# Reading x^T turned straight from HBM, with the first weights on a second DMA queue, at the start of a fused attention and MLP kernel

## The chip, the cores and the metric

The kernel runs on one core of a Trainium2 chip. The metric is device time in microseconds (us) of one execution; the median of several executions is quoted. A profile adds records of one execution, and its own span is shorter than the device time of the same execution (260.0 against 261.42 us for the kernel before).

## The reference, cut to what matters

A linear-attention block and an MLP block read the same x (2048 tokens by 640), and a sigmoid gate mixes them. Only the first products matter here:

```python
x = A_x                                            # 1 x 2048 x 640, bf16
g = sigmoid((x * gate_w).sum(-1, keepdims=True))
qkv = x @ wqkv                                     # q, k, v of 640 columns each
pq, pk = phi(q), phi(k)                            # phi(t) = where(t > 0, t + 1, exp(t)) + 1e-6
...
return g * a + (1 - g) * b
```

The kernel computes q = x @ wq with x^T (features on partitions) as the stationary operand: in the trace of the kernel before, the q and k steps load 128x128 blocks of xT (LDWEIGHTS, 98 ns in the median) and multiply them with 512 and 128 to 131 columns of wq or wkg. In all, 16 tiles of 128 tokens must be turned.

## The kernel before

The program puts the loads of the start on SyncE's one queue, in about the order of need (a tiny "touch" of the weights on ScalarE's queue apart). Tiles 0 to 3 of x come plain and are turned by TensorE (five 128x128 transposes a tile, then a VectorE copy out of PSUM). Tiles 4 to 15 are turned by DMA transposes that read x_tok in SBUF.

```python
dma_in(x_tok[:, 0, :], x2[0:128, :], "x0")         # dma_in: SyncE's queue
dma_in(x_tok[:, 1, :], x2[128:256, :], "x1")
load_wq(0)
dma_in(x_tok[:, 2:4, :], x2[256:512, :].rearrange("(n p) d -> p n d", p=128), "x23")
for k in range(1, KD):                             # KD = 5 slices of 128 rows
    load_wq(k)
for k in range(KD):
    dma_in(wkg[:, k, 0:D], A_wqkv[128 * k:128 * (k + 1), D:2 * D], "wk%d" % k)
dma_in(wkg[:, :, D + 2:D + 3], gate_w..., "gw", noncontig=True)
for c in range(1, NCH):
    dma_in(x_tok[:, 4 * c:4 * c + 4, :], ..., "xc%d" % c)
    for t in range(4 * c, 4 * c + 4):
        sch.dma("sp", xT[:, :, 128 * t:128 * (t + 1)], x_tok[:, t, :], "trx%d" % (t % 4), transpose=True)
```

TensorE fills the wait for the first data with a warm-up of dummy matmuls, then interleaves transposes and the steps (tile, k) of q, so that no step needs a slice of wq long before it lands:

```python
WARM = 3200                                        # columns of dummy matmuls
addA(("warm",), 0.0, lambda: warmup(WARM, 0.834))
... transposes of tiles 0 and 1, two more dummies ...
order = [(0, 0), (None, None), (1, 0), (2, None), (3, None), (0, 1), (1, 1), (2, 0), (0, 2), (1, 2), (3, 0),
         (0, 3), (1, 3), (0, 4), (2, 1), (1, 4), (2, 2), (2, 3), (2, 4), (3, 1), (3, 2), (3, 3), (3, 4)]
```

Here (t, None) is the turning of tile t and (None, None) a dummy. After q of tiles 0 to 3 comes k of tile 0 in five steps, and then k of tile 1, which is the first tile of the ordinary kind; its start serves below as the end of the lead-in.

## Time and profile before

| | before |
|---|---|
| median time | 262.2 us (261.58 to 262.69, 4 runs) |
| TensorE busy | 254.7 of 260.0 us |
| first ordinary k tile starts | 12.6 us |
| from there to the end of the span | 247.4 us |

The page's span, its line of TensorE (PE; busy us, share of the span, instructions), and the first line of the chain that ended last:

```profile
span 260.0 us, 4263 instructions
PE 254.7 (98%) x1671; PEld 135.9 (52%) x1703; DVE 148.9 (57%) x266; ACT 106.9 (41%) x215; POOL 96.8 (37%) x151
...
PE 97%; issue 1%; DVE 1%; POOL 0%; POOLq 0%
```

The view of waits for TensorE (who waited for whom: us in total, times, longest):

```profile
PE ps L830 <- POOL xn L659: 1.1, 1, 1.1
PE ps L1106 <- issue: 0.5, 3, 0.2
```

TensorE is the limit, and beyond 0.5 us of issue it waits for nothing but the memset that feeds its warm-up. So there is little to win but the lead-in. The timeline shows that lead-in (start us, us, engine, line, operation, out<-in, shape, count, idle time before):

```profile
1.05 2.85 PE L830 MATMUL ps<-xn 128*128 128x512 bf16 x7 [1.05 <-POOL xn L659]
3.69 1.21 PE L611 MATMUL ps<-ident,x_tok 128*128 128x128 bf16 x10
...
5.11 0.38 PE L857 MATMUL ps<-wq,xT 128*128 128x512 bf16 x1
...
7.14 0.38 PE L857 MATMUL ps<-wq,xT 128*128 128x512 bf16 x1
7.41 0.38 PE L857 MATMUL ps<-wq,xT 128*128 128x512 bf16 x1
...
12.63 4.26 PE L600 MATMUL ps<-wkg,xT 128*128 128x512 bf16 x29
```

L830 is the warm-up, L611 the transposes, L857 the 512-column part of a q or k step (the other 128 columns follow). A duration of 0.38 us and a spacing of 0.27 us between steps are full speed here: the clock records of this trace put the rise to a granted clock of 1.00 at 4.7 us. The 25 steps before the ordinary k tile make 25 x 0.27 = 6.8 us, so 5.8 us of the 12.6 are lead-in.

The table of stretches (us; busy us and instructions of TensorE, its weight load, VectorE, ScalarE and GpSimd; last three columns: granted TensorE clock, DMA share, GB/s) shows the DMA engines full with plain loads from 4 us on:

```profile
4.00:6.00 2.00, 1.90 (x23) 1.49 (x21) 0.96 (x2) 0.00 (x0) 0.26 (x3) 1.00 1.03 350
6.00:8.00 2.00, 2.00 (x22) 1.29 (x20) 0.89 (x2) 0.00 (x0) 0.00 (x0) 1.00 1.04 340
```

The DMA transposes of this kernel, all from SBUF (durations of issue in ns, then us from issue to landing):

```profile
L281 SPq DMA_TRANSPOSE xT<-x_tok x12: 1200/1276/1595, 13.2 to 39.2; - x12
...
DMA to landing us min/median/max: 2.6/3.7/6.6
```

### The profile page before, as it was taken

What the parts mean: (1) busy time and instruction counts of PE and PEld (TensorE: products, weight loads), DVE (VectorE), ACT (ScalarE), POOL (GpSimd) and SP (SyncE); (2) the same over time, 40 slices, a digit from 0 to 9 for tenths busy, and PEclk for the clock granted to TensorE, in tenths of its full rate; (3) what the DMA queues carried; (4) which work ended last, traced back from release to release, by engine and by line L of the source; (5) the groups of instructions that cost most, each with busy time, mean ns of one, the idle gap of its engine ahead of it and who ended that gap; (6) DMA issues with size and microseconds to landing.
All of it is one profiled execution on the core that took longest, in us unless ns stands there. A gap on an engine that the chain in (4) does not pass through costs nothing.

```text
span 260.0 us, 4263 instructions
## 1 busy us (share of the span) xinstructions
PE 254.7 (98%) x1671; PEld 135.9 (52%) x1703; DVE 148.9 (57%) x266; ACT 106.9 (41%) x215; POOL 96.8 (37%) x151
## 2 busy tenths in 40 slices
PE   8999999999999999999999999999999999999996
PEld 4555555555555454555444545554455544455553
DVE  1597877899903799979994407992033410143333
ACT  1496777741355757674874240005500045100000
POOL 5013995859874017865854202230011100021001
PEclk9999999999999999999999999999999999999999
DMA  6855989642566894355565700232000020000311
GB/s 199 255 103 143 211 149 158 194 87 23 105 126 103 275 377 94 76 101 58 107 124 109 125 0 0 45 85 74 3 0 0 3 101 0 3 0 0 103 50 50
DMA packets 50691, 24.82 MB, mean 95 GB/s; under 512 B 42052, under 2 KB 49261, under 8 KB 50672
## 3 DMA queue, kind: packets, MB, share of 16 engines
q1 hardware_dynamic: 49280, 21.15, 35.8%
q0 software_dynamic: 1152, 3.28, 5.2%
q8 instruction: 13, 0.21, 0.3%
q10 hardware_dynamic: 240, 0.13, 0.2%
q14 instruction: 6, 0.05, 0.1%
HBM read 12.05 MB, written 2.62 MB: 56 GB/s over the span
## 4 chain that ended last, share of the span: by engine, by line
PE 97%; issue 1%; DVE 1%; POOL 0%; POOLq 0%
PE ps L600 61%; PE ps L1106 21%; PE ps L781 8%; PE ps L857 2%; PE ps L830 1%; PE ps L1020 1%; PE ps L1088 1%; DVE x_tok L639 1%; PE ps L858 1%; PE ps L611 1%; PE ps L934 1%; PE ps L1085 0%; POOL xn L659 0%; POOLq L1249 0%
## 5 line engine op out<-in xcount | busy, mean ns | idle before, releaser
L600 PE MATMUL ps<-xnT,w 128*128 128x512 bf16 x349 | 80.7, 379 | 0.5
L1106 PE MATMUL ps<-w,h2T 128*128 128x128 bf16 (+1 forms) x409 | 57.9, 298 | 0.7 <-issue 0.5
L656 ACT ACTIVATE h2T<-ps 128x512 bf16<-128x512 f32 x52 | 30.5, 600 | 65.6 <-PE ps L600 65.5
L600 PEld LDWEIGHTS ps<-xnT,w 128*128 128x128 bf16 x360 | 33.9, 98 | 36.9 <-issue 0.4
L639 DVE SCALAR_TENSOR_TENSOR x_tok<-ps,stg,abx 128x512 bf16<-128x512 f32 (+1 forms) x32 | 17.2, 551 | 61.6 <-PE ps L1106 61.6
L622 POOL TENSOR_SCALAR abx<-x_tok,stg 128x640 f32<-128x640 bf16 x16 | 14.8, 923 | 100.6 <-DVE x_tok L639 95.1
L1106 PEld LDWEIGHTS ps<-w,h2T 128*128 128x128 bf16 x416 | 32.4, 98 | 25.6 <-issue 1.1
L622 POOL TENSOR_SCALAR xn<-x_tok,st 128x640 bf16<-128x640 bf16 x32 | 36.8, 1155 | 15.4 <-DMA xnT<-xn 14.9
L656 ACT ACTIVATE Er<-ps 128x640 bf16<-128x640 f32 x32 | 22.4, 704 | 17.4 <-PE ps L600 8.5
L655 ACT ACTIVATE junk<-x_tok 128x640 bf16<-128x640 bf16 x32 | 23.6, 737 | 4.9 <-DVE x_tok L637 4.4
L656 ACT ACTIVATE hsT<-ps 128x512 bf16<-128x512 f32 (+1 forms) x32 | 18.9, 593 | 15.1 <-PE ps L600 12.7
L600 PE MATMUL ps<-w,hsT 128*128 128x512 bf16 (+1 forms) x159 | 23.8, 298 | 0.1
L600 PE MATMUL ps<-M_sb,pqnT 128*128 128x128 bf16 (+1 forms) x156 | 23.5, 297 | 0.3
L781 PE MATMUL ps<-pk_tok,x_tok 128*128 128x128 bf16 (+1 forms) x156 | 23.3, 297 | 0.2
L639 DVE SCALAR_TENSOR_TENSOR abx<-ps,stg,abx 128x640 f32<-128x640 f32 x16 | 14.1, 884 | 15.3 <-PE ps L600 15.3
L600 PE MATMUL ps<-wkg,xT 128*128 128x512 bf16 (+1 forms) x147 | 22.3, 298 | 0.2
L600 PEld LDWEIGHTS ps<-w,hsT 128*128 128x128 bf16 x160 | 13.3, 98 | 12.3
L600 PEld LDWEIGHTS ps<-M_sb,pqnT 128*128 128x128 bf16 x160 | 13.1, 98 | 10.4
L600 PE MATMUL ps<-wq,xT 128*128 128x512 bf16 (+1 forms) x119 | 18.2, 298 | 0.1
L622 DVE TENSOR_SCALAR Er<-Er 128x640 bf16<-128x640 bf16 x32 | 12.0, 376 | 9.1 <-ACT Er L656 8.8
L637 DVE SCALAR_TENSOR_TENSOR x_tok<-ps,x_tok 128x640 bf16<-128x640 f32 x16 | 13.1, 821 | 6.9 <-PE ps L600 6.0
L600 PEld LDWEIGHTS ps<-wkg,xT 128*128 128x128 bf16 x150 | 12.2, 97 | 9.0
(71 smaller groups left out, 230.0 us busy)
## 6 DMA issues: line engine op xcount, KB each, us to landing
w<-in_B_w_dram SPq DMA_DIRECT2D x1, 2160.0 KB, 8.2
w<-in_B_w_dram SPq DMA_DIRECT2D x1, 2080.0 KB, 13.7
x_tok<-in_A_x_dram SPq DMA_DIRECT2D x3, 640.0 KB, 5.7
out_dram<-x_tok SPq DMA_DIRECT2D x3, 640.0 KB, 3.5
w<-in_B_w_dram POOLq DMA_DIRECT2D x8, 160.0 KB, 4.8
wq<-in_A_wqkv_dram SPq DMA_DIRECT2D x5, 160.0 KB, 3.8
wkg<-in_A_wqkv_dram SPq DMA_DIRECT2D x5, 160.0 KB, 3.9
wv<-in_A_wqkv_dram POOLq DMA_DIRECT2D x1, 800.0 KB, 6.2
```

The costliest lines, as they stand in the source:

```text
L600: ins = e.matmul(out_ap, l, r, start=(i == 0), stop=(i == n - 1))
L611: ins = e.transpose(o, s_, ident[:])
L622: return engf(lambda e: e.tensor_scalar(out_ap, in_ap, s1, s2, op0, op1), rd, [out_ap], cost=cost)
L637: return dve(lambda e: e.scalar_tensor_tensor(out_ap, in0, scalar, in1, op0, op1, accum_out=accum), rd, [out_ap, accum], cost=cost + 70.0)
L639: return dve(lambda e: e.scalar_tensor_tensor(out_ap, in0, scalar, in1, op0, op1), rd, [out_ap], cost=cost)
L655: return act(lambda e: e.activation(out_ap, in_ap, func, bias=bias, scale=scale, accum_out=accum), rd, wr, cost=cost)
L656: return act(lambda e: e.activation(out_ap, in_ap, func, bias=bias, scale=scale), rd, wr, cost=cost)
L781: ins = e.matmul(o, l, r, start=(t0 + q_ == 0), stop=(t0 + q_ == NT - 1))
L830: ins = e.matmul(ps[:, b, 0:n], xn[:, 0, 0:128], xn[:, 0, 0:128].unsqueeze(1).to_broadcast([128, n // 128, 128]), start=True, stop=True)
L857: e.matmul(ps[:, b, 0:512], l, w[:, k, 0:512], start=(k == 0), stop=(k == KD - 1))
L858: return e.matmul(ps[:, b + 1, 0:n2], l, w[:, k, 512:512 + n2], start=(k == 0), stop=(k == KD - 1))
L1106: ins = e.matmul(o, l, r, start=False, stop=(i == KFF - 1), skip_group_check=(n0 > 0))
```

## The change

The intent is to take x's turning off TensorE altogether: all 16 tiles are read turned from HBM on SyncE's queue, wq and wk go out beside them on ScalarE's queue, and x itself follows behind, since only later work needs it. The warm-up reads a constant set before the start barrier; the gate's column is turned by a tiny matmul. Cut to its core:

```diff
-    dma_in(x_tok[:, 0, :], ...) ... load_wq ... wk ... xc ... trx from x_tok
+    def load_w(dst, name, k, c0):
+        sch.dma("act", dst[:, k, 0:D], A_wqkv[128 * k:128 * (k + 1), c0:c0 + D], "%s%d" % (name, k))
+    def x_turned(t):
+        sch.dma("sp", xT[:, :, 128 * t:128 * (t + 1)], x2[128 * t:128 * (t + 1), :], "trx%d" % (t % 4), transpose=True)
+    sch.dma("pool", gwr[0:KD, :], gate_w.rearrange("(k p) -> k p", p=128), "gw")
+    for t in range(4):
+        x_turned(t)
     for k in range(KD):
-        dma_in(wkg[:, k, 0:D], ...)
+        load_w(wq, "wq", k, 0)
+    for k in range(KD):
+        load_w(wkg, "wk", k, D)
+    for c in range(NCH):
+        x_chunk(c)
+        for t in range(4 + 3 * c, 7 + 3 * c):
+            x_turned(t)
...
-    WARM = 3200
-    WARM2 = 256
+    WARM = 3712
...
-        order = [(0, 0), (None, None), (1, 0), (2, None), (3, None), (0, 1), ... ]
+        order = [(t, k) for t in range(4) for k in range(KD)]
+        order.insert(KD, (None, None))             # here: the gate's matmul
```

More of the change, by code (lines that the diff above doesn't have):

```diff
@@ L464, in psb @@
         return ps[:, b, :].bitcast(BF16)[:, n0:n1]
-    ones_c = pa.alloc("ones_c", [128, 768], BF16)
+    ones_c = pa.alloc("ones_c", [128, 128], BF16)
     ident = pa.alloc("ident", [128, 128], BF16)
@@ L470, in _build @@
     negh = pa.alloc("negh", [128, 4], F32)
+    gwr = pa.alloc("gwr", [8, 128], BF16)
     st1 = pa.alloc("st1", [128, 8, NT], F32)
@@ L674, in dma_in, with x_chunk @@
         return sch.dma("sp", out_ap, in_ap, key, **kw)
-    sch.dma("act", junk[0:16, 0, 0:80].rearrange("p (k f) -> p k f", k=KD),
-            A_wqkv[:, 0:16].rearrange("(k e r) f -> e r k f", k=KD, r=8)[:, 0, :, :], "touch")
-    dma_in(x_tok[:, 0, :], x2[0:128, :], "x0")
-    dma_in(x_tok[:, 1, :], x2[128:256, :], "x1")
-    def load_wq(k):
-        dma_in(wq[:, k, :], A_wqkv[128 * k:128 * (k + 1), 0:D], "wq%d" % k)
-    load_wq(0)
-    dma_in(x_tok[:, 2:4, :], x2[256:512, :].rearrange("(n p) d -> p n d", p=128), "x23")
-    for k in range(1, KD):
-        load_wq(k)
-    for k in range(KD):
-        dma_in(wkg[:, k, 0:D], A_wqkv[128 * k:128 * (k + 1), D:2 * D], "wk%d" % k)
-    dma_in(wkg[:, :, D + 2:D + 3], gate_w.rearrange("(k p o) -> p k o", p=128, o=1), "gw", noncontig=True)
-    for c in range(1, NCH):
-        dma_in(x_tok[:, 4 * c:4 * c + 4, :], x2[512 * c:512 * (c + 1), :].rearrange("(n p) d -> p n d", p=128), "xc%d" % c)
-        for t in range(4 * c, 4 * c + 4):
-            sch.dma("sp", xT[:, :, 128 * t:128 * (t + 1)], x_tok[:, t, :], "trx%d" % (t % 4), transpose=True)
+    def load_w(dst, name, k, c0):
+        sch.dma("act", dst[:, k, 0:D], A_wqkv[128 * k:128 * (k + 1), c0:c0 + D], "%s%d" % (name, k))
+    def x_turned(t):
+        sch.dma("sp", xT[:, :, 128 * t:128 * (t + 1)], x2[128 * t:128 * (t + 1), :], "trx%d" % (t % 4), transpose=True)
+    def x_chunk(c):
+        dma_in(x_tok[:, 4 * c:4 * c + 4, :], x2[512 * c:512 * (c + 1), :].rearrange("(n p) d -> p n d", p=128), "xc%d" % c)
+    sch.dma("pool", gwr[0:KD, :], gate_w.rearrange("(k p) -> k p", p=128), "gw")
+    for t in range(4):
+        x_turned(t)
+    for k in range(KD):
+        load_w(wq, "wq", k, 0)
[5 more added lines that the diff above has]
+            x_turned(t)
     k_done = {}
@@ L716, in load_wvo @@
             sch.dma("pool", wo_aug[0:n, r, :], A_wo[R6 * r:R6 * r + n, :], "wo", group_total=6, deps=dp)
-    memset(pool, xn[:, 0, 0:128], 1.0)
     memset(pool, ones_c[:], 1.0)
@@ L740, in _build, with gate_turn @@
     IT = _Items()
-    WARM = 3200
-    WARM2 = 256
-    def t_x(t):
+    WARM = 3712
+    def gate_turn():
         b = bank()
-        tr_group(b, [x_tok[:, t, 128 * k:128 * (k + 1)] for k in range(KD)])
-        src = psb(b, 0, D).rearrange("p (k c) -> p k c", k=KD)
-        dst = xT[:, :, 128 * t:128 * (t + 1)]
-        copy(dve, dst, src)
+        pe(lambda e: e.matmul(ps[:, b, 0:KD], gwr[0:KD, :], ident[0:KD, 0:KD], start=True, stop=True),
+           [gwr[0:KD, :], ident[:]], [ps[:, b, 0:KD]], cost=60.0)
+        copy(dve, wkg[:, :, D + 2:D + 3], ps[:, b, 0:KD].rearrange("p (k o) -> p k o", o=1))
     def phi(b, dst, after_exp=None):
@@ L829, in fn @@
             for n in steps:
-                ins = e.matmul(ps[:, b, 0:n], xn[:, 0, 0:128], xn[:, 0, 0:128].unsqueeze(1).to_broadcast([128, n // 128, 128]), start=True, stop=True)
+                ins = e.matmul(ps[:, b, 0:n], nc.const_aps.tensor(1.0, [128, 128], BF16), nc.const_aps.tensor(1.0, [128, n], BF16),
+                               start=True, stop=True)
             return ins
-        pe(fn, [xn[:, 0, 0:128]], [ps[:, b, :]], cost=cols * cyc)
+        pe(fn, [], [ps[:, b, :]], cost=cols * cyc)
     def q_tile(t):
@@ L844, in stream @@
             if k is None:
-                if t is None:
-                    warmup(256, 0.42)
-                else:
-                    t_x(t)
+                gate_turn()
                 continue
@@ L864, in q_four @@
     def q_four():
-        order = [(0, 0), (None, None), (1, 0), (2, None), (3, None), (0, 1), (1, 1), (2, 0), (0, 2), (1, 2), (3, 0), (0, 3), (1, 3), (0, 4),
-                 (2, 1), (1, 4), (2, 2), (2, 3), (2, 4), (3, 1), (3, 2), (3, 3), (3, 4)]
+        order = [(t, k) for t in range(4) for k in range(KD)]
+        order.insert(KD, (None, None))
         stream(order, wq, 128, lambda t, b: phi(b, pq_tok[:, t + 1, :]))
@@ L879, in _build @@
     addA(("warm",), 0.0, lambda: warmup(WARM, 0.834))
-    for i in range(2):
-        addA(("tx", i), 0.28, lambda i=i: t_x(i))
-    addA(("warm", 1), 0.0, lambda: warmup(WARM2, 0.42))
     addA(("q", 3), 5.44, q_four)
```

## The prediction

> **What bounds it now.** TensorE. The page has PE busy 254.7 of 260.0 us (98%), the chain of waits is 97% PE, and the waits view gives PE 1.1 us at the start (for GpSimd's memset) and 0.5 us of issue, nothing else. From 12 to 53 us every stretch of the busy table shows PE at 9.9 of 10 us. So only the lead-in can be won.
>
> **The lead-in.** In the timeline the k tiles of the ordinary kind start at 12.6 us. Before them lie 25 dense steps (20 of wq, 5 of wkg), one each 0.27 us when TensorE is at speed: 6.8 us. So the kernel pays 12.6 - 6.8 = 5.8 us before dense work: warm-up 2.85 us from 1.05, 20 x transposes (1.21 + 0.72 us), four small warm-up matmuls, and gaps of 0.2 to 0.3 us.
>
> **Removed:** 20 TensorE transposes and 4 filler matmuls; 4 DVE copies (1.9 us, not critical); the memset wait (the warm-up now reads a constant set before the start barrier: 0.25 us earlier); the twelve waits of the transposing DMAs for x_tok. **Added:** 4 more DMA transposes, all reading HBM; one tiny gate matmul with a DVE copy. **Moved:** wq and wk to ScalarE's queue, ten issues of about 0.45 us, so the table load comes near 5 to 6.6 us, still before the first exp. Later engine orders are the same apart from the start.
>
> **Cost of the new start.** A DMA transpose takes 1.28 us to issue (median of 12) and 2.6 to 3.7 us to land. If HBM ones are alike, tiles 0 to 3 land at about 4, 5.3, 6.6 and 8 us; TensorE eats one per 1.36 us, so they keep up. The weights decide. Tile 0 now runs k=0..4 at once and needs all of wq 1.1 us after it starts; before, x transposes and other tiles filled that time. In the busy table the DMA is full at about 350 GB/s for weights but 200 GB/s for transposes, so a turned tile costs about 0.8 us of all 16 engines (estimate) and wq 2.3 us. [...] Wq shared with two or three turned tiles from about 2.1 us is in at about 6 to 7.3 us. That sets the dense start at 5.0 to 6.2 us, against 5.8. Expected gain 0.5 us, all on the chain; nothing comes back later, as PE stays full.
>
> **Risk.** [...] here matmuls reach full speed at about 5.1 us after a start at 1.05. The new warm-up ends near 3.9 us and then TensorE waits for DMAs[...].
>
> **Prediction:** 261.5 us, 80% range 259.9 to 263.0; faster by over 2%: 0.01, within 2%: 0.96, slower by over 2%: 0.03.
>
> **What would show it.** Right: the timeline has warm-up from about 0.8 us, then TensorE waiting for xT and then wq DMAs, the first ordinary k tile at 11.8 to 12.8 us; DMA share near 1 from 3 to 11 us; after 13 us PE full as before, all later phases shifted by the same amount. Wrong: waits of PE for xT or wkg DMAs after 8 us; ScalarE waiting for x_tok chunk 0 in its square, backing PSUM up; half-speed matmuls (0.43 us apart) beyond 5.5 us.
>
> **What would make it wrong.** HBM transposes landing much later than SBUF ones (3 us each would cost 5 us or more); issuing much faster, with tiles crowding out wq; weights winning the interleave, so that x lands late.

The sum stands: 5.0 to 6.2 us before dense work against 5.8, a gain put at 0.5 us. That two queues share the engines, on which its time for wq rests, was an assumption; the packet records below fit it (58 and 103 GB/s from 4 to 9 us).

## The result and the profile after

The changed kernel takes 264.7 us (264.53 to 265.96, 4 runs) against 262.2: the ratio is 1.011, with a 95% interval of 1.0077 to 1.0143. A ratio here is the mean time of one kernel's fast runs over that of the other's in the same rounds, so it is not quite the ratio of the medians. The change is slower by 2.5 us, clear of noise though under 2%, and outside the range predicted.

The page after, the same lines:

```profile
span 264.7 us, 4244 instructions
PE 259.0 (98%) x1681; PEld 135.0 (51%) x1681; DVE 148.7 (56%) x263; ACT 107.3 (41%) x215; POOL 94.3 (36%) x151
...
PE 95%; DMA 2%; ACTq 1%; DVE 1%; issue 0%
```

PE's share of busy time has not moved, although the kernel does less on TensorE and takes longer. Time on the chain has gone to DMA and to ScalarE's issuing. The waits of TensorE now:

```profile
PE ps L855 <- DMA xT<-in_A_x_dram: 1.9, 1, 1.9
PE ps L830 <- PEq L1244: 0.8, 1, 0.8
PE ps L855 <- DMA wq<-in_A_wqkv_dram: 0.7, 1, 0.7
```

The timeline of the lead-in:

```profile
0.83 3.25 PE L830 MATMUL ps<-const-bfloat16-1.0 128*128 128x512 bf16 x8 [0.83 <-PEq L1244]
6.03 0.59 PE L855 MATMUL ps<-wq,xT 128*128 128x512 bf16 x1 [1.95 <-DMA xT<-in_A_x_dram]
...
8.44 0.61 PE L855 MATMUL ps<-wq,xT 128*128 128x512 bf16 x1 [0.65 <-DMA wq<-in_A_wqkv_dram]
...
12.14 0.63 PE L855 MATMUL ps<-wq,xT 128*128 128x512 bf16 x1
12.67 0.63 PE L855 MATMUL ps<-wq,xT 128*128 128x512 bf16 x1
13.21 0.52 PE L855 MATMUL ps<-wq,xT 128*128 128x512 bf16 x1
13.62 0.38 PE L855 MATMUL ps<-wq,xT 128*128 128x512 bf16 x1
...
17.16 4.26 PE L601 MATMUL ps<-wkg,xT 128*128 128x512 bf16 x30
```

Two things stand out. TensorE runs dry at about 4 us and waits for turned tile 0. And from 6 to 13.3 us steps come 0.53 us apart, with durations of 0.6 us: half speed, which is counted as busy (the run with the weights held back, below, shows the same durations beside a recorded clock of 0.50). The column of the granted clock does not show it, since it reads 1.00 until the first recorded change of the clock, here at 13.5 us; the spacing of matmuls does.

The first ordinary k tile starts at 17.2 us in place of 12.6, and from there it is 247.5 us to the end, as before (247.4). So the whole loss lies in the lead-in. The two profiled executions overstate it: that of before, at 261.42 us, was one of its fastest, and that of after, at 265.96 us, its slowest.

The DMA engines in the same stretches, and the transposes:

```profile
4.00:6.00 2.00, 0.08 (x1) 0.00 (x0) 0.00 (x0) 0.00 (x0) 0.84 (x5) 1.00 1.09 159
6.00:8.00 2.00, 1.76 (x6) 0.65 (x6) 0.00 (x0) 1.17 (x1) 0.00 (x0) 1.00 1.25 176
8.00:10.00 2.00, 1.45 (x5) 0.35 (x5) 0.00 (x0) 0.11 (x1) 0.00 (x0) 1.00 1.09 189
```

```profile
L281 SPq DMA_TRANSPOSE xT<-in_A_x_dram x16: 1199/1280/3270, 0.8 to 28.4; - x16
...
DMA to landing us min/median/max: 3.6/5.2/9.7
```

From 4 to 10 us the engines are as full as before (share over 1) but move 159 to 189 GB/s where they moved 340 to 350. (From 2 to 4 us, at a share of 1.04, they moved 266, and from 10 to 14 us 218 and then 306.) To issue a transpose costs the same (1.28 us); to land takes 5.2 us in the median. The semaphore records of the trace put the landings at:

| landed at (us) | tile 0 | tile 1 | tile 2 | tile 3 | wq 0 | wq 4 | wk 4 |
|---|---|---|---|---|---|---|---|
| before (x plain) | 3.4 | 3.6 | 5.7 | 5.7 | 4.8 | 7.9 | 10.4 |
| after | 5.9 | 9.2 | 11.1 | 13.5 | 3.4 | 9.2 | 14.9 |

The prediction had the tiles at 4, 5.3, 6.6 and 8 us.

### The profile page after: what moved, and what is told of

It reads as the page before. It is cut to its first block, busy times and chain, and to the rows that moved or that the text cites. A ratio compares the mean times of both kernels' runs of the same rounds, so it can differ in the third digit from the quotient of the medians.

```text
span 264.7 us, 4244 instructions
## 1 busy us (share of the span) xinstructions
PE 259.0 (98%) x1681; PEld 135.0 (51%) x1681; DVE 148.7 (56%) x263; ACT 107.3 (41%) x215; POOL 94.3 (36%) x151
## 4 chain that ended last, share of the span: by engine, by line
PE 95%; DMA 2%; ACTq 1%; DVE 1%; issue 0%
PE ps L601 60%; PE ps L1101 21%; PE ps L781 8%; PE ps L855 2%; DMA wq<-in_A_wqkv_dram 2%; PE ps L1015 1%; PE ps L1083 1%; ACTq L285 1%; DVE x_tok L640 1%; PE ps L856 1%; PE ps L929 1%; PE ps L1080 0%; PE ps L747 0%
## 5 line engine op out<-in xcount | busy, mean ns | idle before, releaser
L601 PE MATMUL ps<-xnT,w 128*128 128x512 bf16 x360 | 82.3, 379 | 0.0
L1101 PE MATMUL ps<-w,h2T 128*128 128x512 bf16 (+1 forms) x416 | 58.8, 299 | 0.0
L640 DVE SCALAR_TENSOR_TENSOR x_tok<-ps,stg,abx 128x512 bf16<-128x512 f32 (+1 forms) x32 | 17.2, 551 | 61.7 <-PE ps L1101 61.6
L623 POOL TENSOR_SCALAR xn<-x_tok,st 128x640 bf16<-128x640 bf16 x32 | 33.4, 1051 | 13.4 <-DMA xnT<-xn 12.9
L601 PE MATMUL ps<-M_sb,pqnT 128*128 128x512 bf16 (+1 forms) x160 | 24.4, 299 | 0.0
L781 PE MATMUL ps<-pk_tok,x_tok 128*128 128x512 bf16 (+1 forms) x160 | 23.9, 299 | 0.0
L640 DVE SCALAR_TENSOR_TENSOR abx<-ps,stg,abx 128x640 f32<-128x640 f32 x16 | 14.1, 883 | 13.5 <-PE ps L601 13.5
L601 PEld LDWEIGHTS ps<-w,hsT 128*128 128x128 bf16 x160 | 13.3, 98 | 12.3
L601 PEld LDWEIGHTS ps<-M_sb,pqnT 128*128 128x128 bf16 x160 | 13.1, 98 | 10.4
```

Source lines behind the costliest of these rows:

```text
L601: ins = e.matmul(out_ap, l, r, start=(i == 0), stop=(i == n - 1))
L623: return engf(lambda e: e.tensor_scalar(out_ap, in_ap, s1, s2, op0, op1), rd, [out_ap], cost=cost)
L640: return dve(lambda e: e.scalar_tensor_tensor(out_ap, in0, scalar, in1, op0, op1), rd, [out_ap], cost=cost)
L781: ins = e.matmul(o, l, r, start=(t0 + q_ == 0), stop=(t0 + q_ == NT - 1))
L1101: ins = e.matmul(o, l, r, start=False, stop=(i == KFF - 1), skip_group_check=(n0 > 0))
```

## The experiments

Three theories. **C, the clock:** the gap after the warm-up keeps TensorE at half speed for longer. **D1:** a transpose from HBM is slow in itself or beside any plain load. **D2:** with weights on a second queue the engines no longer serve loads in the order of need: wk, wanted last, is moved in the same microseconds as the turned tiles, wanted first. The changed kernel's packet records show both queues moving data from 4 to 9 us, 1138 packets of turned tiles (58 GB/s) and 403 of weights (103 GB/s), and its landings fit D2: wk 0 to 2 were in at 10.5, 11.5 and 13.2 us, before turned tile 3 at 13.5.

### Long warm-up on the changed kernel

```diff
-    WARM = 3712
+    WARM = 7168
```

> The changed kernel with a warm-up of 7168 columns in place of 3712 and nothing else: TensorE stays busy until the first turned tile lands near 6 us. Theory C (the clock: the gap after the warm-up leaves TensorE at half speed until 13.3 us): matmuls at full speed from the first wq step, the first ordinary k tile near 14.9 us in place of 17.1, total about 262.5 to 263.3 us. Theory D (the data: turned tile 0 and wq 3 and 4 land late, and that alone sets the start): total unchanged at 264.5, or worse where filler stands in the way.

Measured: 264.5 us (264.29 to 265.35), ratio 1.0081 (1.0045 to 1.0116). The dummies ran on to 5.7 us and the clock stepped up during them, by its records at 4.5 us:

```profile
0.83 4.98 PE L830 MATMUL ps<-const-bfloat16-1.0 128*128 128x512 bf16 x14 [0.83 <-PEq L1244]
5.74 0.38 PE L855 MATMUL ps<-wq,xT 128*128 128x512 bf16 x1
...
12.90 0.39 PE L855 MATMUL ps<-wq,xT 128*128 128x512 bf16 x1 [0.93 <-DMA xT<-in_A_x_dram]
...
15.64 2.61 PE L601 MATMUL ps<-wkg,xT 128*128 128x512 bf16 x15
```

Every q step is at full speed, and yet the total is not to be told from that of the changed kernel. The time that full speed saved was spent waiting: turned tile 3 landed at 12.85 us, and the ten steps behind it take 2.7 us more. Theory C alone falls; so does the idea that C has no part, as the square of runs below shows.

### Short warm-up on the kernel before

```diff
-    WARM = 3200
+    WARM = 1024
```

> The kernel before with its warm-up cut from 3200 to 1024 columns, no DMA touched. Theory C: a gap of about 1.7 us before the first transposes is enough to delay the step to full speed [...], so total 263 to 265.5 us with half-speed matmuls to 8 us or later. Theory D: the data land as before, so the total stays within 0.5 us of 262.2.

Measured: 263.3 us (263.13 to 263.47) against 262.3 in the same rounds; the ratio, 1.0029 (0.9989 to 1.0068), does not exclude equality, because one run of before in these rounds was at 264.64. The profile is plainer: the first ordinary k tile starts at 14.5 us, and the steps stay at half speed until 9 us with no DMA changed:

```profile
7.96 0.63 PE L857 MATMUL ps<-wq,xT 128*128 128x512 bf16 x1
8.49 0.63 PE L857 MATMUL ps<-wq,xT 128*128 128x512 bf16 x1
9.03 0.40 PE L857 MATMUL ps<-wq,xT 128*128 128x512 bf16 x1
```

A gap of 1.3 us, from 2.1 to 3.4 us, went with a step to full speed at 9 us in place of 5, at a price of about 1 us in the medians; all four runs lie above ten of the eleven of the kernel before. Since the step also varies from run to run with the same warm-up (4.6 us in the next run, 13.5 in the changed kernel), one profile does not show how much of the delay is the gap's.

### Weights held back until the first four turned tiles have landed

```diff
-    for t in range(4):
-        x_turned(t)
+    first_four = [x_turned(t) for t in range(4)]
...
-        sch.dma("act", dst[:, k, 0:D], ..., "%s%d" % (name, k))
+        sch.dma("act", dst[:, k, 0:D], ..., "%s%d" % (name, k), deps=first_four)
```

> The changed kernel with wq and wk held back until the first four turned tiles have landed: a measurement, slower on purpose. If a transpose from HBM is as cheap as one from SBUF, the four land about 1.3 us apart, 2.6 to 3 us after issue, the last near 7.5 us. If a transpose from HBM is by itself dearer, they land 4 us or more after issue, and the DMA share is near 1 with nothing else running. If only sharing with the weights made tile 0 land at 6.0 us, it lands now near 3.5 us. Total 266 to 270 us.

One look: 274.04 us, its state unknown as for any single run; only the landings and rates are used. Alone, the four tiles landed at 4.6, 5.7, 7.0 and 7.8 us, 3.0 to 3.8 us after issue and as fast as they can be issued. The stretches:

```profile
4.00:6.00 2.00, 0.08 (x1) 0.00 (x0) 0.00 (x0) 0.00 (x0) 0.84 (x5) 1.00 0.69 128
6.00:8.00 2.00, 0.00 (x0) 0.00 (x0) 0.00 (x0) 0.00 (x0) 0.00 (x0) 1.00 0.69 128
...
12.00:14.00 2.00, 0.72 (x2) 0.13 (x2) 0.00 (x0) 0.48 (x1) 0.00 (x0) 0.50 1.22 191
```

Two steps of its timeline:

```profile
20.74 0.63 PE L854 MATMUL ps<-wq,xT 128*128 128x512 bf16 x1
...
21.73 0.38 PE L854 MATMUL ps<-wq,xT 128*128 128x512 bf16 x1
```

So a transpose from HBM by itself keeps up with its issue, as predicted; tile 3 at 13.5 us in the changed kernel is the work of the company it keeps. The 128 GB/s are the pace of issue, 160 KB every 1.28 us. Dividing them by the share (128 / 0.69 = 186) does not give what full engines would move: where turned tiles wait in a row behind a larger load, as from 24.5 to 25.5 us of this same run, they move 287 GB/s by themselves at a share of 1.28, by the packet records. That is less than the 340 to 350 of plain loads, but far more than the 159 to 189 of the changed kernel's mixture.

The third stretch shows the clock as the trace records it: 0.50, after TensorE had been idle from 4.1 us on. The clock records put its rise at 4.6 us, its fall at 8.0 and its next rise at 21.6, on the two sides of which the two steps shown took 0.63 and 0.38 us. So 0.63 us is half speed. Mark the rise at 4.6 us: the warm-up is that of the changed kernel to the instruction, and there the clock rose at 13.5. With the same warm-up, ending at 4.1 us, the step thus came at times 8.9 us apart.

### Only the weights moved to ScalarE's queue, on the kernel before

```diff
-    sch.dma("act", junk[0:16, 0, 0:80]..., "touch")
     dma_in(x_tok[:, 0, :], ...); dma_in(x_tok[:, 1, :], ...); dma_in(x_tok[:, 2:4, :], ...)
-    wq and wk slices: dma_in(...)
+    wq and wk slices: sch.dma("act", ...)
```

> The kernel before with only the weights moved to ScalarE's queue (and its small touch DMA left out); x still comes plain and is turned by TensorE. Theory D says that the transposes from HBM are what is late, not the weights' queue: the same as before or up to 0.5 us faster, 261.7 to 262.3 us, with wq 4 landing before 7 us. If the move to ScalarE's queue were what hurts, 263.5 us or more.

Measured: 263.2 us (262.56 to 263.49), ratio 1.002 (0.9991 to 1.0049). The expectation missed: with no transpose from HBM at all, x tiles 2 and 3 landed at 7.5 us in place of 5.7 and wq 4 at 10.0 us in place of 7.9, and TensorE waited 1.1 us for x. The interval of the ratio reaches from 0.1% faster to 0.5% slower, so a loss in total time is not shown. But the two other runs that left the loads of the kernel before alone (the short warm-up and the early start) had x tiles 2 and 3 at 6.3 and 6.4 us and wq 4 at 8.1, so the landings show that a second queue costs order by itself.

### wk behind the turned tiles on SyncE's queue

```diff
     for k in range(KD):
-        load_w(wkg, "wk", k, D)
+        dma_in(wkg[:, k, 0:D], A_wqkv[128 * k:128 * (k + 1), D:2 * D], "wk%d" % k)
```

> The changed kernel with one thing different: the five wk loads go out on SyncE's queue behind the first four turned tiles, so that beside those tiles only wq is on ScalarE's queue. Theory D2 (the second queue lets weights that nobody needs yet share the 16 DMA engines with the turned tiles, and that is what makes tile 3 land at 13.5 us in place of the 7.8 us it takes alone): tile 3 lands near 9 to 10.5 us, the first ordinary k tile at 13.3 to 14.5 us, total 262 to 263.3 us. Rival D1 (a transpose from HBM beside any plain load is slow, whichever): tile 3 still near 12 us or later, total 264 us or more.

Measured: 264.5 us (263.79 to 265.76), ratio 1.0087 (1.0057 to 1.0117). Half of D2's expectation came: tiles 2 and 3 landed at 9.2 and 9.8 us in place of 11.1 and 13.5. Tiles 0 and 1, at 6.3 and 8.8 us, were no earlier to speak of than in the changed kernel (5.9 and 9.2): for them wq alone is company enough, so D1's "beside any plain load" holds in part. The total did not move:

```profile
6.44 0.58 PE L855 MATMUL ps<-wq,xT 128*128 128x512 bf16 x1 [2.36 <-DMA xT<-in_A_x_dram]
...
9.99 0.47 PE L855 MATMUL ps<-wq,xT 128*128 128x512 bf16 x1
...
15.27 2.90 PE L601 MATMUL ps<-wkg,xT 128*128 128x512 bf16 x20
```

Now no tile but the first is waited for, and what is left is the clock: half speed until 10.2 us in this execution. The mirror image of the long warm-up.

### Both: wk behind, and a long warm-up

```diff
     (wk as in the run before)
-    WARM = 3712
+    WARM = 6656
```

> The run before it (wk behind the turned tiles) with a warm-up of 6656 columns too. If the clock's loss comes out now that data are earlier (theory C with D2): 0.5 to 1.5 us faster than that run, 261.3 to 262.3 us. If the data alone bind, the same within 0.4 us.

Measured: 263.1 us (262.61 to 263.21), ratio 1.0025 (1.0004 to 1.0046).

```profile
6.25 0.38 PE L855 MATMUL ps<-wq,xT 128*128 128x512 bf16 x1
...
7.95 0.39 PE L855 MATMUL ps<-wq,xT 128*128 128x512 bf16 x1 [0.71 <-DMA wq<-in_A_wqkv_dram]
...
14.46 3.76 PE L601 MATMUL ps<-wkg,xT 128*128 128x512 bf16 x24
```

The gain of 1.4 us over the run with wk behind alone was in the range expected, though the total stayed above it. The four runs make a square of medians, in us:

| | warm-up 3712 | long warm-up |
|---|---|---|
| wk beside the tiles | 264.7 | 264.5 |
| wk behind the tiles | 264.5 | 263.1 |

Each repair alone is worth 0.2 us, within noise; both are worth 1.6, and every run with both (the slowest at 263.21) is faster than every run of the other three (the fastest at 263.79). The lower row was run later than the upper, and on another chip than the long warm-up; the kernel before had a median of 262.2 to 262.3 us each time. The late data and the slow clock cover the same microseconds, so taking away one lays bare the other. What remains, 0.9 us over the kernel before, is seen in the wait for wq at 7.95 us: tiles and wq were all in at 9.6 us here, against 7.9 us for the plain loads of the same bytes.

### All loads on one queue, in the order of need

```diff
     (the load helper issues on SyncE's queue)
-    four turned tiles | wq, wk beside them
+    x_turned(0); wq 0 to 4; x_turned(1), (2), (3); wk 0 to 4
```

> The changed kernel with all loads on SyncE's queue in the order of need: turned tile 0, wq 0 to 4, turned tiles 1 to 3, wk, then as before. The order in which data land is then the order of issue. D2: tile 0 near 4 us, wq 4 near 6.5 us, tile 3 near 10.5 us (issue takes 1.28 us a tile and 0.45 us a slice, 7.5 us in all), first ordinary k tile at 13.5 to 14.5 us, total 262.3 to 263.3 us: slightly behind the kernel before, with issue time as the limit. D1: 264 us or more.

Measured: 264.3 us (263.94 to 265.16), ratio 1.0079 (1.0055 to 1.0103). The landings came much as D2 said, in the order of issue: tile 0 at 4.0, wq 4 at 7.6 (6.5 was expected), tile 3 at 10.3 us. The total did not, since the steps stayed at half speed until 13.2 us and the first ordinary k tile started at 16.5.

With the warm-up lengthened to 6144 columns:

> All loads on SyncE's queue in the order of need, as in the earlier run of that kind, with the warm-up lengthened from 3712 to 6144 columns. There the profile had tile 0 at 4.0 us, wq 4 at 7.6 and tile 3 at 10.3, but half-speed matmuls to 13.2 us and a first ordinary k tile at 16.5. If the clock was what kept it at 264.3 us: first ordinary k tile at 14.3 to 14.8 us, total 262.8 to 263.4 us. If not: 264 us or more.

Measured: 263.9 us (263.16 to 264.31), ratio 1.0051 (1.0024 to 1.0078), a miss by half a microsecond. In the profile the first ordinary k tile came at 14.7 us, as expected, but it was 248.3 us from there to the end in place of 247.4: with all on one queue x itself landed only at 17.6 us, and TensorE then waited 0.7 us for VectorE's evacuation of k. That the late x caused this is argued from the order of the loads, not tested; in the run before it x came as late (17.6 us), k 1.8 us later, and nothing was lost.

### An attempt to beat both

```diff
     (kernel before; touch DMA left out)
+    wq 0 to 4 on ScalarE's queue
     x tiles 0, 1 plain on SyncE's queue
+    x_turned(2), x_turned(3) on SyncE's queue, then wk, then x tiles 2 and 3 plain
+    order: (0, k), (1, k) interleaved, then tiles 2 and 3
```

> An attempt to beat both: the kernel before with tiles 0 and 1 plain and turned by TensorE, tiles 2 and 3 turned from HBM behind them on SyncE's queue, wq on ScalarE's queue, wk on SyncE's queue after the turned tiles. Saves ten transposes (0.7 us) on TensorE. If wq on a queue of its own does not hold up tiles 2 and 3 beyond 8 us: 261.5 to 262.0 us. If sharing does hold them up as D2 would have it for any two queues: 262.5 to 263.5 us.

Measured: 262.8 us (262.68 to 263.88), ratio 1.0027 (1.0005 to 1.0048). It does not beat the kernel before, and lies where D2 had put it. wq 4 landed at 8.3 us and tiles 2 and 3 at 8.5 and 8.9, steps ran at half speed until 6.5 us, and half a microsecond went on waiting for VectorE to free PSUM.

### Plain x, wq on ScalarE's queue, wk behind x

```diff
     (as the run with only the weights moved)
-        load_w(wkg, "wk", k, D)
+        dma_in(wkg[:, k, 0:D], ..., "wk%d" % k)
```

> The kernel before with x plain and turned by TensorE, wq on ScalarE's queue, and wk on SyncE's queue behind x: it differs from the run with all weights on ScalarE's queue only in where wk goes, so that no second queue carries what is not needed yet. D2 (a second queue lets wk share the engines with x and wq): x tiles 2 and 3 land before 6.5 us in place of 7.5, wq 4 before 8 us in place of 10 to 12, total 262.0 to 262.6 us against 263.2. If the queue of wk made no difference: 263.2 us.

Measured: 263.0 us (262.0 to 265.86), ratio 1.0047 (1.0005 to 1.0089): not to be told from 263.2, and the landings missed what was expected. x tiles 2 and 3 came at 7.1 us and wq 4 at 9.7. wk on SyncE's queue, issued from 2.2 us on since plain x takes little time to issue (0.44 us a tile in the kernel before, against 1.28 for a turned one), could now share the engines with wq on the other, and x still shared with wq. That it is not the name of the queue that counts, but whether what is wanted later shares with what is wanted first, is argued from these times, not tested.

### The early start alone, on the kernel before

```diff
-    memset(pool, xn[:, 0, 0:128], 1.0)
...
-    e.matmul(ps[:, b, 0:n], xn[:, 0, 0:128], ...)
+    e.matmul(ps[:, b, 0:n], nc.const_aps.tensor(1.0, [128, 128], BF16), nc.const_aps.tensor(1.0, [128, n], BF16), ...)
```

> The kernel before with one part of the change, the warm-up reading the constant that is set before the start barrier, so that TensorE starts at 0.83 us and not at 1.05. If an earlier start alone brings the step to full speed earlier on average: 0.1 to 0.3 us faster, 261.9 to 262.2 us. If the arrival of x tile 0 at 3.4 us sets everything: no difference.

Measured: 262.4 us (261.91 to 264.03), ratio 1.0016 (0.9988 to 1.0044): no gain to be seen. No version run here beats the kernel before.

## Why the prediction was wrong

- **Right: what bounds the kernel, and that only the lead-in matters.** In ten of the eleven timed or profiled variants and in both kernels it is 247.4 to 247.6 us from the first ordinary k tile to the end. All that the variants won or lost was won or lost before it. (The exception is the long warm-up on one queue.)
- **Right in its terms:** a transpose from HBM issues like one from SBUF (1.28 us) and, alone, lands 3.0 to 3.8 us after issue.
- **The step that failed:** "If HBM ones are alike, tiles 0 to 3 land at about 4, 5.3, 6.6 and 8 us; TensorE eats one per 1.36 us, so they keep up. The weights decide." The tiles landed at 5.9, 9.2, 11.1 and 13.5 us. The prediction let the tiles slow wq down, but let the tiles themselves land as if alone. Beside wq they do not: with wk moved away tiles 0 and 1 still came at 6.3 and 8.8 us, against 4.6 and 5.7 alone. And it left out that wk, issued on the second queue from 3.5 us on, would share with tiles 2 and 3: with wk behind them tile 3 came at 9.8 us. What that did to the dense start is seen where the clock is out of the way, in the long warm-up: TensorE waited for tile 3, and 15.6 - 6.8 = 8.8 us went before dense work, where 5.0 to 6.2 was predicted.
- **The rate was mis-sized.** A turned tile and a plain slice were added up as if each kept its own rate, 200 and 350 GB/s. Together they moved 159 to 189 GB/s from 4 to 10 us with the share at 1.09 or more, which is slower than either kind by itself (turned tiles in a row 287, plain loads 340 to 350). That wq would be in at 6 to 7.3 us was thus too early by 2 to 3 us (9.2). The packet records of the traces say where the time goes: plain loads move in packets of 1280 bytes, which took 60 ns in the mean before (4 to 8 us) and 148 ns beside turned tiles (4 to 9 us); turned tiles move in packets of 256 bytes, which took 21 ns with the weights held back (3 to 7 us) and 29 ns beside plain loads. Why the mixture is so slow was not found out.
- **The clock was named as a risk and left out of the middle of the range.** It came true. In the profiled execution full speed came at 13.5 us, not 5.1. The step varied from run to run: with a busy lead-in the first rise is recorded at 4.7 us (before), 4.5 and 6.2 us (two long warm-ups), and with the warm-up of the changed kernel at 4.6 (weights held back), 10.2 (wk behind) and 13.5 us. What sets it was not shown. With the weights held back the records lie 3.41 us (rise to fall) and 13.65 us (fall to rise) apart. And the records of the changed kernel's five executions fall in two kinds: a granted clock of 0.994 with 264.5 to 264.8 us, and 1.00 with 265.3 and 266.0. An estimate from the shorter of those two distances: 3.41 us at half speed take 0.5 x 3.41 / 263 = 0.6% off the mean clock, which is what 0.994 lacks of 1 (so probably it rose early, as with the weights held back, and fell back for about that long; these executions left no trace to look at); in the profile of the other kind the clock rose at 13.5 us and nothing fell before. The profile thus shows the worse of two cases, by 0.5 to 1.4 us.
- **The sum was the wrong form.** The prediction kept a data term and a clock term apart, as if each had its own price. The square of runs shows that they overlap: 0.2 us for either repair, 1.6 us for both. The remaining 0.9 us stays when both are repaired; that it is the engines' longer work on turned reads is argued from landings and rates, not shown by a run of its own.

## What to carry to other kernels

Where one queue delivers loads in the order of need, a second queue added no bandwidth here (plain loads on two queues: 179 and 270 GB/s in the first two fortieths of the span, against 199 and 255 on one), and what was waited for came later (wq 4 at 10.0 us against 7.9); so put on it only what is wanted at the same time. Let a warm-up last until the first real data: in the profile of the changed kernel a pause of 1.95 us after it was followed by half speed until 13.5 us, and in that with 7168 columns every step ran at full speed. And half-speed matmuls counted as busy (2.00 of 2.00 us from 10 to 12 us, with steps 0.53 us apart), so read their spacing and not the busy share. When undoing a cause changes nothing, undo the other suspect together with it before giving it up: two limits that cover the same time hide each other.
